# First batch of a spectral mixing layer: its transposes as whole 112 by 128 blocks and six steps ahead, the weights' sums on VectorE, half of y's writes on ScalarE's queue

## The chip, the core and the metric

The kernel runs on one core of one Trainium2 chip. The metric is device time in microseconds (us) for one execution. The engines named below are TensorE (PE, with PEld for its weight loads), VectorE (DVE), ScalarE (ACT), GpSimd (POOL) and SyncE (SP). SP, ACT and POOL also issue DMA transfers, each through a queue of its own.

## The reference

The reference filters a sequence in the frequency domain and passes the result through a two-layer network with an ELU between the layers. `x` (8 batches, 3008 steps, 256 channels) and the two filter parts (1505 frequencies, 256 channels) are float32. `w_in` (256 by 2048) and `w_out` (2048 by 256) are float64.

```python
X = np.fft.rfft(x, axis=1)
Y = X * (filt_r + 1j * filt_i)[None, :, :]
y = np.fft.irfft(Y, n=3008, axis=1).astype(np.float32)
h = y.reshape(8 * 3008, 256) @ w_in
g = np.where(h > 0.0, h, np.exp(np.minimum(h, 0.0)) - 1.0)
out = (g @ w_out).astype(np.float32)
```

## The kernel before

**The transform.** 3008 is 47 times 64, so each Fourier transform is done as matmuls in two steps with tables of cosines and sines. For a batch the stages are: first step (`a_*`), a change of layout, second step (`b_*`), the product with the filter, and the same two steps back (`bi_*`, `n_*`). Batches 1 to 7 change layout through a scratch tensor `z` in HBM. Batch 0 has functions of its own (`a_first`, `t_first`, `b_first`, `bi_first`) that change layout on chip by transposing with TensorE, so that the kernel can start without the round trip.

**The network.** The second layer's work is cut into 192 quads: for each of 8 batches, 6 blocks `m` of rows, and for each block 4 quarters `q` of the 2048 hidden channels. A quad does the "ups" (`w_in`, ELU) and, one quad later, the "downs" (`w_out`). All blocks but the first use seven products for a two by two block product, for which sums of weight blocks are needed (`w_sums`, L955: four dependent add or subtract operations of 128 by 256 each, for every second weight chunk; the last of the four overwrites the block `a21`). The first block of batch 0 (quads 0 to 3, `plain_ups` and `plain_downs`) does eight plain products and needs no sums; quad 4 is the first to read them, of `w_in[0]`, and quad 5's step reads those of `w_out[0]`.

**The weights.** They arrive as pairs of 32-bit words in 16 chunks (`w_fetch`), and are turned into float32 by DVE and ACT: `w_split` (L914, L915, two DVE operations), `w_float` (L925, three ACT operations), `w_join` (L929, L939, then L947 or L953, on DVE). The first chunks are converted during batch 0's transform, the rest during quads 0 to 3.

**The order.** The program is written out by hand (`manual_schedule`). Each engine works through its own list in order and waits on semaphores. What an engine does next is set by the order of the calls in the code. Batch 0's opening (from L977) is:

- loads of `x`, tables, the filter (`ff`, in two halves of eight rows: L1021 to L1024, on SP and POOL) and weights;
- `a_table` (DVE) and six `a_first`, with one warming matmul (`warm(1, 256)`, L1055, on data that nobody reads) after each of the first five;
- `t_first(0)`, `t_first(1)`, the first weight chunk (`step(0)`), `t_first(2)`, `t_first(3)`;
- a loop over g = 0 to 9 (L1065): `b_first(g)` for g below 8 with the four filter products on DVE (L407 to L410), `bi_first(g - 2)` in the middle of it from g = 2 on, `t_first(g + 4)` for g below 4, pieces of weight conversion at fixed g, and from g = 2 on `y_write_first(g - 2)`, two DMA transfers, one on SP's queue and one on POOL's (on ACT's for the last g);
- `y_read` (L1089, SP), the rest of the early weights, eight warming matmuls, and `n_unit(0, 0)`, with which the network begins.

`t_first(g)` (L332) writes four psum tiles in turn (`po0` to `po3`, two of them per g), each copied out by an ACT operation (L349). The destination `t` is one of `t2` (g 0 and 1), `t4p` (2 and 3) and `xp` (4 to 7); the last are the buffers in which `x` came. `b_first` takes two of the four banks `m0` to `m3` and gives them back after the products. `bi_first` uses `po0` to `po3` as well (L431).

Work at fixed points of the later quads is entered with `at(quad, place, function, ...)` (L1118). Within a quad the places come in the order 2, 3, 0, 4, 5, 1: 2 and 3 between its first seven steps, 0 in its middle, 4 and 5 between the last steps, 1 at its end. The weights' sums stand there (L1139), with POOL as engine, in quads 1 to 5. `x_unit` (L235) of batch 1, four DVE operations per pair of chunks, stands at place 0 of quads 3, 4 and 5; `a_unit` follows at place 1.

Of the kernel before, what the change touches and what calls it, by code (L numbers as in the profile page):

```python
# [11 lines left out]
FP32 = mybir.dt.float32  # L12
U32 = mybir.dt.uint32
AXT = mybir.ActivationFunctionType
# [12 lines left out]
P = 128  # L27
# [6 lines left out]
NXC = H // XC  # L34
NG = K2 // 4
# [3 lines left out]
HALVES = slice(0, 64), slice(64, 128)  # L39
# [103 lines left out]
def kernel(  # L143
# [9 lines left out]
    nc = tc.nc  # L153
# [6 lines left out]
    def pool(name, bufs, **kw):  # L160
        return ctx.enter_context(tc.tile_pool(name=name, bufs=bufs, **kw))
# [15 lines left out]
    psO = pool("psO", 1, space=PSUM)  # L177
# [105 lines left out]
    zt = [[], [w[3].rearrange("p a b c -> p (a b c)") for w in (w_in, w_out)]]  # L283
    ROWS = 112
# [32 lines left out]
    def a_first(c):  # L317
        xt, w = xs.pop((0, c)), tas.pop((0, c))
        for dh in range(2):
            k, ps = bank("psa", (P, 64, XC, 2))  # L320
            for u in range(XC):
                nc.tensor.matmul(ps[:, :, u, :], xt[:, u, ts(dh, P)], w[:, u, :].rearrange("p (k q) -> p k q", q=2),  # L322
                                 start=True, stop=True)
            for kh in range(2):
                z = zt[kh][dh]
                o = bass.AP(tensor=z.tensor, offset=z.offset + 2 * XC * c,
                            ap=[list(z.ap[0]), [ROWS, 16], [64, 2], [1, 2 * XC]])
                s = ps[:, 32 * kh:32 * kh + 32].rearrange("p (k a) u q -> p k a (u q)", a=2)
                nc.scalar.activation(out=o, in_=s, func=AXT.Copy)
            banks.append(k)  # L330

    def t_first(g):  # L332

        if g < 2:
            t = t2[:, g]
        elif g < 4:
            t = t4p.tile([P, 4, D], FP32, tag="t4", name="tf")
        else:
            t = xp.tile([P, 2, 2, D], FP32, tag="xc", name="tf").rearrange("p k u d -> p (k u) d")
        t2s[0, g] = t  # L340
        ps = [psO.tile([P, 4, 2, 64], FP32, tag="po%d" % i, name="po%d" % i) for i in range(2 * (g % 2), 2 * (g % 2) + 2)]
        for k in range(4):
            for dh in range(2):
                for o, n in ((0, 64), (64, ROWS - 64)):
                    for r, p in zip(HALVES, ps):
                        nc.tensor.matmul(p[o:o + n, k, dh, :], zt[k // 2][dh][r, (2 * g + k % 2) * ROWS + o:(2 * g + k % 2) * ROWS + o + n],  # L346
                                         eye[r, r], start=True, stop=True)
        for h, p in enumerate(ps):
            nc.scalar.activation(out=t[0:ROWS].rearrange("p k (e h f) -> p k e h f", e=2, h=2)[:, :, :, h], in_=p[0:ROWS], func=AXT.Copy)  # L349

# [59 lines left out]
    def b_first(g, f, pq, between):  # L412
        t = t2s.pop((0, g))
        (i0, re), (i1, im) = (bank(n) for n in ("psr", "psi"))
        for o, a in ((0, 0), (64, 2)):
            for ps, k in ((re, LO), (im, HI)):
                tile_mm(ps[o:o + 64], gf, k, [t[:, a:a + 2, :]], g == 0 and a == 0)
        if between:
            between()
        products(re, im, f, *pq)  # L420
        banks.extend((i0, i1))

        sr, si, p, q = pq
        ss[0, g] = [sr, p], [si, q]

    def bi_first(g):
        s = ss.pop((0, g))
        t = t3s[0, g] = (t2 if g % 4 > 1 else t3f)[:, g % 2]

        pa, pb = (psO.tile([P, 2, 256], FP32, tag="po%d" % i, name="po%d" % i)  # L430
                  for i in ((0, 1) if g > 2 and g % 2 else (2, 3)))  # L431
        for o, table, sv in ((0, gr, s[0]), (64, gi, s[1])):
            for ps, k in ((pa, LO), (pb, HI)):
                tile_mm(ps[o:o + 64], table, k, sv, g == 0 and k == LO)
        nc.scalar.activation(out=t[:, 0:2, :], in_=pa, func=AXT.Copy)
        nc.scalar.activation(out=t[:, 2:4, :], in_=pb, func=AXT.Copy)

    def y_write_first(g, queues=(nc.sync, nc.sync)):
        if g == 0:
            yds[0] = yd.tile([K2, 96, D], FP32, tag="yd", name="yd")  # L440
        t = t3s.pop((0, g))
        for a, r in enumerate((LO, HI)):
            queues[a].dma_start(yds[0][4 * g:4 * g + 4, 48 * a:48 * a + 48, :].rearrange("u r d -> r u d"), t[r])
# [467 lines left out]
    def w_split(k):  # L911
        m, e = wts[k] = wtmp[TEMPS[k]]
        hi = wds[k][:, :, 1]
        nc.vector.tensor_scalar(out=m, in0=hi, scalar1=0x000FFFFF, scalar2=None, op0=ALU.bitwise_and)  # L914
        nc.vector.tensor_scalar(out=e, in0=hi, scalar1=0x7FF00000, scalar2=None, op0=ALU.bitwise_and)  # L915

    def w_float(k, *parts):

        m, e = wts.get(k, (None, edges.bitcast(U32)))
        ef, l = e.bitcast(FP32), wds[k][:, :, 0]  # L920
        steps = [(l.bitcast(FP32), l, AXT.Identity, 2.0 ** -52, 1.0),
                 (ef, e, AXT.Relu, -8.0, edges[:, 0:1]), (e, ef, AXT.Relu, -1.0, edges[:, 1:2])]
        for i in parts or range(3):
            o, x, func, scale, bias = steps[i]
            nc.scalar.activation(out=o, in_=x, func=func, scale=scale, bias=bias)  # L925
# [51 lines left out]
    with tc.manual_schedule():  # L977


        with tc.tile_pool(name="boot", bufs=1) as bp:  # L980
            ff = bp.tile([P, 2, 2 * NG, D], FP32, name="ff")
            once = bp.tile([P, 2, P], FP32, name="once")
            eye, gf = once[:, 0], once[:, 1].rearrange("p (v q) -> p v q", v=2)
# [15 lines left out]
            def warm(n, w=512):  # L999
                ps = psO.tile([P, 512], FP32, tag="po3", name="warm")  # L1000
                for k in range(n):
                    nc.tensor.matmul(ps[:, 0:w], rq[:, 0, 0, 0:P], rq[:, 0].rearrange("p u d -> p (u d)")[:, 0:w], start=True, stop=True)
# [35 lines left out]
            k = kp.tile([P, 2, 2, 256], FP32, tag="k", name="wme").rearrange("p i u d -> p i (u d)")  # L1038
            places(k[:, 0], k[:, 1])
            c = kp.tile([P, 2, 512], FP32, tag="c", name="wme")  # L1040
# [3 lines left out]
            def step(k):  # L1044
                w_split(k)
                w_float(k)
                if k > 0 and k - 1 in wds:
                    w_join(k - 1)
# [2 lines left out]
                a_table(c)  # L1051
            for c in range(NXC):
                a_first(c)
                if c < NXC - 1:
                    warm(1, 256)  # L1055
            for g in range(2):
                t_first(g)
            step(0)
            for g in range(2, 4):
                t_first(g)  # L1060
            w_join(0)
            w_fetch(4, nc.gpsimd)
# [2 lines left out]
            for g in range(NG + 2):  # L1065
                back = (lambda g=g: bi_first(g - 2)) if g >= 2 else None
                if g < NG:
                    b_first(g, [ff[:, c, 2 * g:2 * g + 2] for c in range(2)], pqs[g % 2], back)
                else:
                    back()  # L1070
                if g < 4:
                    t_first(g + 4)
                if g == 1:
                    w_split(1)
                    w_float(1)
                if g == 2:
                    w_join(1)
                    w_fetch(5, nc.gpsimd)
                if g == 3:
                    w_split(2)  # L1080
                if 4 <= g < 7:
                    w_float(2, g - 4)
                if g == 6:
                    w_split(3)
                if g == 7:
                    w_float(3, 0)
                if g >= 2:
                    y_write_first(g - 2, (nc.sync, nc.scalar if g == NG + 1 else nc.gpsimd))
            y_read(0, 0, slice(0, K2 - 4), slice(K2 - 4, K2))  # L1089
            w_join(2)  # L1090
            w_fetch(6)
# [26 lines left out]
        def at(quad, place, fn, *a):  # L1118
            plan.setdefault((quad, place), []).append((fn, a))
# [16 lines left out]
        for quad, *counts in ((0, 1, 1, 1, 1, 1, 1, 1, 0), (1, 1, 1, 1, 1, 1, 1, 1, 1), (2, 1, 1, 1, 1, 1, 1, 1, 1), (3, 1, 1, 1, 0, 0, 0, 0, 0)):  # L1136
            for n, count in enumerate(counts):
                plan.setdefault((quad, 7 + n % 2, *BLOCKS[n // 2]), []).append((convert, (count,)))
        for quad, place, k in ((1, 2, 1), (2, 2, 3), (2, 0, 5), (3, 2, 7), (3, 0, 9), (4, 2, 11), (4, 0, 13), (5, 2, 15)):  # L1139
            at(quad, place, w_sums, k, nc.gpsimd)  # L1140
        for c, (quad, place) in enumerate(((2, 0), (2, 1), (2, 1), (2, 1))):
            at(quad, place, x_load, 1, c)
        at(0, 1, nc.sync.dma_start, pairs, pairs_d)
# [6 lines left out]
        for b in range(B):  # L1150
            t = (b - 1) * PER
# [109 lines left out]
```

## Time and profile before

| | us |
|---|---|
| median of 3 timed runs | 2559.62 |
| the three runs | 2555.52, 2559.62, 2561.19 |
| the profiled execution | 2552.35 |
| its span, from first to last instruction | 2550.5 |
| busy PE, PEld, DVE, ACT, POOL | 2520.4, 2167.4, 2105.0, 1509.4, 173.0 |

Busy times are shares of one execution; engines work side by side, so they do not add up. A gap of the engine that is on the path costs time, a gap of another engine does not. "Who waited for whom" names the engine and line that waited, what released it, the total in us, how often, and the longest wait. A table of windows gives for each stretch (us from the span's start) its length, then the busy time and the number of instructions of each engine, the granted TensorE clock (1.00 is full), the mean busy share of the DMA engines (about 1 is saturated) and GB/s. A timeline line gives start, duration, engine, line, operation, names, shape and count, and in brackets the idle time ahead of it and what ended it. L346 is line 346 of the kernel before.

### The profile page before, as it was taken

To read this page: it belongs to the slowest core of one execution; us is meant where nothing else is said; L and a number is where in the kernel's file an instruction comes from. 1 tells how busy PE (TensorE), PEld (TensorE's weight loads), DVE (VectorE), ACT (ScalarE), POOL (GpSimd) and SP (SyncE) were. 2 spreads that over 40 slices of the span, in tenths; PEclk is the share of its full clock that TensorE was granted. 3 is DMA by queue.
4 is the path that set the end of the run, shared out by engine and by line. 5 is a ranking of instruction groups with operands and counts; after the bars stand their busy time and mean duration, and the time that the engine had idled before them with its cause. 6 is when DMAs were issued, how large, how long until landed. Compare 5 with 4: busy or idle time off the path is not lost.

```text
span 2550.5 us, 46325 instructions
## 1 busy us (share of the span) xinstructions
PE 2520.4 (99%) x17766; PEld 2167.4 (85%) x17766; DVE 2105.0 (83%) x3607; ACT 1509.4 (59%) x2652; POOL 173.0 (7%) x325
## 2 busy tenths in 40 slices
PE   7899999999999999999999999999999999999999
PEld 5788889888898888988889888888889888898887
DVE  4968897888888888888888898788897888876766
ACT  4755565656556565565555656556655665555554
POOL 3310000000000000000000000000010001000000
PEclk9999999999999999999999999999999999999999
DMA  8653213512234232342224321343223322111010
GB/s 205 198 158 83 57 42 88 135 47 72 47 86 120 58 73 54 91 101 66 59 51 124 86 71 36 77 116 82 57 48 91 83 53 69 38 45 29 9 28 17
DMA packets 226671, 194.43 MB, mean 76 GB/s; under 512 B 127914, under 2 KB 199306, under 8 KB 226258
## 3 DMA queue, kind: packets, MB, share of 16 engines
q1 hardware_dynamic: 212722, 161.39, 25.8%
q0 software_dynamic: 13232, 29.62, 4.2%
q8 instruction: 140, 2.29, 0.4%
q14 instruction: 81, 0.66, 0.1%
q10 hardware_dynamic: 496, 0.46, 0.1%
HBM read 119.51 MB, written 74.97 MB: 76 GB/s over the span
## 4 chain that ended last, share of the span: by engine, by line
PE 95%; DVE 2%; DMA 1%; issue 1%; ACT 1%; SPq 1%; POOL 0%; ACTq 0%; DVEq 0%; POOLq 0%
PE po L816 44%; PE phs L730 25%; PE phd L730 12%; PE pha L730 6%; PE psn L608 2%; PE pf L458 1%; PE pv L525 1%; PE psa L254 1%; PE po L402 1%; PE po L690 0%; SPq L866 0%; PE po L346 0%; PE psa L322 0%; DMA t<-tf_t 0%; PE psr L402 0%
## 5 line engine op out<-in xcount | busy, mean ns | idle before, releaser
L816 PE MATMUL po<-g,wo 128*128 128x256 f32 (+1 forms) x5264 | 1293.8, 377 | 0.0
L816 PEld LDWEIGHTS po<-g,wo 128*128 128x128 f32 x5264 | 990.8, 190 | 165.3 <-issue 51.7
L741 ACT ACTIVATE g<-phs 128x512 f32<-128x512 f32 (+1 forms) x564 | 332.2, 589 | 743.4 <-PE phs L730 743.3
L748 ACT ACTIVATE e<-e 128x512 f32<-128x512 f32 (+1 forms) x752 | 468.1, 623 | 23.9
L738 DVE TENSOR_TENSOR g<-phd,g 128x512 f32<-128x512 f32 (+1 forms) x376 | 254.4, 677 | 198.7 <-ACT e L748 120.0
L752 DVE SCALAR_TENSOR_TENSOR g<-e,g 128x512 f32<-128x512 f32 (+1 forms) x564 | 380.2, 674 | 14.2 <-ACT e L748 14.1
L730 PE MATMUL phs<-y,wi 128*128 128x256 f32 (+1 forms) x1504 | 380.0, 375 | 0.0
L730 PE MATMUL phd<-y,wi 128*128 128x256 f32 (+1 forms) x1488 | 376.0, 375 | 0.4 <-DVE g L738 0.4
L747 ACT ACTIVATE e<-g 128x512 f32<-128x512 f32 (+1 forms) x564 | 347.1, 615 | 36.0 <-DVE g L738 29.2
L730 PEld LDWEIGHTS phs<-y,wi 128*128 128x128 f32 x1504 | 285.6, 190 | 33.0
L730 PEld LDWEIGHTS phd<-y,wi 128*128 128x128 f32 x1488 | 282.2, 190 | 33.7 <-DVE g L738 0.8
L752 DVE SCALAR_TENSOR_TENSOR g<-e,phs 128x512 f32<-128x512 f32 (+1 forms) x188 | 127.2, 677 | 87.2 <-ACT e L748 87.2
L730 PE MATMUL phs<-yb,wi 128*128 128x256 f32 (+1 forms) x752 | 190.2, 375 | 0.3 <-ACT g L741 0.3
L730 PE MATMUL phs<-yt,wi 128*128 128x256 f32 (+1 forms) x752 | 190.0, 375 | 0.0
L730 PE MATMUL pha<-yb,wi 128*128 128x256 f32 (+1 forms) x736 | 185.9, 375 | 0.0
L747 ACT ACTIVATE e<-phs 128x512 f32<-128x512 f32 (+1 forms) x188 | 110.1, 585 | 114.5 <-PE phs L730 114.5
L396 POOL DMA_DIRECT2D fall<-fp x224 | 110.1, 499 | 805.5 <-DVE r L502 797.8
L730 PEld LDWEIGHTS phs<-yb,wi 128*128 128x128 f32 x752 | 140.4, 190 | 19.6 <-ACT g L741 0.7
L738 DVE TENSOR_TENSOR g<-pha,g 128x512 f32<-128x512 f32 (+1 forms) x188 | 126.9, 675 | 36.4 <-PE pha L730 36.4
L730 PEld LDWEIGHTS phs<-yt,wi 128*128 128x128 f32 x752 | 142.8, 190 | 16.5
L730 PEld LDWEIGHTS pha<-yb,wi 128*128 128x128 f32 x736 | 139.8, 190 | 16.1
L791 DVE TENSOR_TENSOR g<-g,g 128x512 f32<-128x512 f32 (+1 forms) x188 | 128.2, 682 | 6.5
(170 smaller groups left out, 2217.6 us busy)
## 6 DMA issues: line engine op xcount, KB each, us to landing
yd<-t SPq DMA_DIRECT2D x120, 192.0 KB
fall<-fp POOLq DMA_DIRECT2D x224, 96.0 KB, 2.9
t<-z SPq DMA_DIRECT2D x224, 96.0 KB
t<-yd SPq DMA_DIRECT2D x84, 256.0 KB
out_dram<-o SPq DMA_DIRECT2D x624, 32.0 KB
z<-t SPq DMA_DIRECT2D x144, 128.0 KB
xc<-in_x_dram SPq DMA_DIRECT2D x84, 128.0 KB
xc<-in_x_dram SPq DMA_DIRECT2D x161, 64.0 KB
```

The lines of the kernel that those rows point to most:

```text
L254: nc.tensor.matmul(ps[k][1][a:a + 32, u, :], w[r, u, 32 * o:32 * o + 32], parts[o][r, u, :], start=True, stop=True, tile_position=(32 * k, a))
L396: nc.gpsimd.dma_start(t[32 * a:32 * a + 24].rearrange("p c u d -> p (c u d)"), fp[g, a].rearrange("q c u d -> q (c u d)"))
L402: nc.tensor.matmul(ps[:, u:u + w, :], table[k, v, :], r[k, u:u + w, :], start=n == 0, stop=n == len(rhs) - 1)
L608: nc.tensor.matmul(o, t[r, i - 4 * m, ds(dh * P + 64 * c, 64)], w[r, i - 4 * m, :], start=True, stop=True)
L730: nc.tensor.matmul(ps[:, a, 0:h], w_in[q][:, COMBO[n], a, :], y[n], start=start and a == 0, stop=True, skip_group_check=True)
L738: nc.vector.tensor_tensor(out=g[o], in0=i0, in1=i1, op=ALU.add)
L741: nc.scalar.activation(out=g[o], in_=i0, func=AXT.Copy)
L747: nc.scalar.activation(out=e, in_=src, func=AXT.Relu, scale=-1.0)
L748: nc.scalar.activation(out=e, in_=e, func=AXT.Exp, scale=-1.0)
L752: nc.vector.scalar_tensor_tensor(out=g[n], in0=es[n], scalar=1.0, in1=src, op0=ALU.subtract, op1=ALU.max)
L791: nc.vector.tensor_tensor(out=b12, in0=b22, in1=b12, op=ALU.subtract)
L816: nc.tensor.matmul(po[i][:, u, 0:h], w_out[q][:, COMBO[n], a, :], g[n][:, a, :], start=q == 0 and a == 0 and n in (1, 3, 6, 4), stop=True, ...
```

## The change

`t_first` transposes a whole block of 112 columns by 128 partitions with one instruction, against the full identity, where it multiplied eight pieces of at most 64 by 64 with a corner of the identity each. For every g that is 8 calls in place of 32. Each psum tile now holds one of the two halves `j`, and ACT copies it out as it stands.

`t_first(0)` to `t_first(5)` are called ahead of the loop (`t_first(0)` to `t_first(3)` before), so the loop's calls are `t_first(6)` and `t_first(7)`. The five warming matmuls between the `a_first` are left out. The second DMA of `y_write_first` goes to ACT's queue for every g. The weights' sums are done by DVE, at other places: quads 3, 4 and 5 only.

```diff
-        ps = [psO.tile([P, 4, 2, 64], FP32, tag="po%d" % i, name="po%d" % i) for i in range(2 * (g % 2), 2 * (g % 2) + 2)]
-        for k in range(4):
-            for dh in range(2):
-                for o, n in ((0, 64), (64, ROWS - 64)):
-                    for r, p in zip(HALVES, ps):
-                        nc.tensor.matmul(p[o:o + n, k, dh, :], zt[k // 2][dh][r, (2 * g + k % 2) * ROWS + o:(2 * g + k % 2) * ROWS + o + n],
-                                         eye[r, r], start=True, stop=True)
-        for h, p in enumerate(ps):
-            nc.scalar.activation(out=t[0:ROWS].rearrange("p k (e h f) -> p k e h f", e=2, h=2)[:, :, :, h], in_=p[0:ROWS], func=AXT.Copy)
+        for j in range(2):
+            i = j + 2 * (g % 2)
+            ps = psO.tile([P, 2, 256], FP32, tag="po%d" % i, name="po%d" % i)
+            for u in range(2):
+                for dh in range(2):
+                    nc.tensor.transpose(ps[0:ROWS, u, ts(dh, P)], zt[j][dh][:, ts(2 * g + u, ROWS)], eye)
+            nc.scalar.activation(out=t[0:ROWS, 2 * j:2 * j + 2, :], in_=ps[0:ROWS], func=AXT.Copy)
...
                 a_first(c)
-                if c < NXC - 1:
-                    warm(1, 256)
             for g in range(2):
                 t_first(g)
             step(0)
-            for g in range(2, 4):
+            for g in range(2, 6):
                 t_first(g)
...
-                if g < 4:
-                    t_first(g + 4)
+                if g < 2:
+                    t_first(g + 6)
...
-                    y_write_first(g - 2, (nc.sync, nc.scalar if g == NG + 1 else nc.gpsimd))
+                    y_write_first(g - 2, (nc.sync, nc.scalar))
...
-        for quad, place, k in ((1, 2, 1), (2, 2, 3), (2, 0, 5), (3, 2, 7), (3, 0, 9), (4, 2, 11), (4, 0, 13), (5, 2, 15)):
-            at(quad, place, w_sums, k, nc.gpsimd)
+        for quad, place, k in ((3, 4, 1), (3, 1, 3), (3, 0, 5), (4, 2, 7), (4, 0, 9), (4, 1, 11), (5, 2, 13), (5, 0, 15)):
+            at(quad, place, w_sums, k)
```

## The prediction

> **What bounds the kernel now.** Read first the page (PE is busy 2520.4 of 2550.5 us), then a table of windows by stage:
>
> ```profile
> 0.00:24.20 24.20, 19.22 (x123) 15.00 (x123) 9.24 (x29) 12.59 (x26) 10.32 (x21) 1.00 0.95 239
> 24.20:35.40 11.20, 4.64 (x248) 4.23 (x249) 2.75 (x5) 5.26 (x10) 5.35 (x10) 0.89 1.03 214
> 35.40:71.30 35.90, 32.37 (x473) 19.05 (x465) 25.83 (x44) 17.85 (x32) 6.97 (x12) 0.89 0.62 172
> ...
> 81.30:133.20 51.90, 45.97 (x242) 43.76 (x243) 46.34 (x77) 35.40 (x62) 23.56 (x26) 1.00 0.57 186
> 133.20:190.00 56.80, 54.49 (x410) 44.78 (x410) 36.20 (x59) 35.25 (x63) 7.40 (x13) 1.00 0.62 165
> 190.00:2550.00 2360.00, 2354.61 (x16257) 2035.75 (x16255) 1974.88 (x3378) 1394.54 (x2449) 117.75 (x242) 1.00 0.28 67
> ```
>
> From 190 us on PE has 5 us free in 2360 and the change leaves that work alone, so the answer lies in the first 190 us. What PE waits for there (PE alone, 0 to 200):
>
> ```profile
> PE po L346 <- issue: 9.1, 3, 5.8
> PE php L663 <- DVE g L672: 4.9, 4, 1.9
> ...
> PE phd L730 <- DVE g L738: 2.0, 1, 2.0
> ...
> PE php L663 <- DVE wi L947: 1.0, 1, 1.0
> ```
>
> The largest has no semaphore behind it: PE stands inside `t_first` with nothing to wait for. Windows cut at these stalls:
>
> ```profile
> 26.30:28.95 2.65, 2.40 (x128) 2.13 (x128) 0.00 (x0) 2.02 (x5) 2.44 (x5) 1.00 0.88 224
> 28.95:34.70 5.75, 0.00 (x0) 0.00 (x0) 1.99 (x3) 2.01 (x4) 1.77 (x4) 0.85 1.07 219
> 34.70:40.75 6.05, 5.96 (x128) 4.47 (x128) 2.80 (x5) 2.17 (x4) 1.73 (x4) 0.58 1.05 208
> 40.75:43.40 2.65, 0.00 (x0) 0.00 (x0) 2.65 (x6) 0.00 (x0) 0.00 (x0) 0.96 0.97 365
> ```
>
> Exactly 128 matmuls and 128 weight loads run between one stall and the next, with the DMA engines full. The DMA view counts one "q8 instruction" packet in 23.4 to 25, one in 29 to 34 and one in 40.7 to 43.4, and the page's queue part gives 2.29 MB over 140 packets, 16 KB each. I read this as PE running out of instructions, whose next block queues behind data. The stalls also cost clock: 0.58 in the third row. [...]
>
> **The change part by part: the opening.** Before, each g has 32 calls of four records (two passes, load and multiply): 512 of each over eight g. The last lines of the kernel (L877) have 8 transposes of 128x128 as 8 matmuls and 8 loads, so one pass. After: 64 of each, 896 instructions fewer, 3.5 blocks. Time: four of L877 take 0.79 us with a 0.29 us tail, 0.15 us apart; a g costs 8 x 0.15 = 1.2 us against 1.7 for its 64 records in 23.65 to 25.3. ACT's copies stay at two of 0.59, 1.1 us a g.
>
> Counting PE and PEld records from the start (246 by 24.2 us), the first stall comes after 449. After, the six `a_first` end at 221, six t_first add 96, and 449 comes in `bi_first(0)`, about 37 us, with its block asked for some 16 us earlier. The next is 256 later, five steps of the loop (48 records each), about 13 us. A block took at most 8 us (from 26.4, when the previous one began, to 34.8). So I expect no stall: 9.1 us go, and the half clock.
>
> What is late next is the filter. Its transfers are on POOL's queue, which the change does not touch until the loop:
>
> ```profile
> 23.97 0.59 POOL L389 DMA_DIRECT2D ff<-in_filt_i_dram  x1 [1.17 <-DMA ff<-in_filt_i_dram]
> ...
> 32.46 0.57 POOL L389 DMA_DIRECT2D ff<-in_filt_i_dram  x1 [1.41 <-DMA ff<-in_filt_i_dram]
> ```
>
> The first half's last transfer goes out at 23.97, and the issue at 32.46 is released by it: 32.5 is the earliest for the first L408. PE is there sooner. x's chunks arrive every 1.8 us (POOL's issues at 13.02 to 19.88 wait for them). `a_first` takes 1.78 us without the 0.43 us of warming and ends near 22; ACT then has 12 copies and 2 us of `w_float`, so t_first(5) and `b_first(0)` are through near 31. Whatever `a_first` and the transposes win is hidden behind the filter.
>
> ```profile
> 37.49 0.69 DVE L407 TENSOR_TENSOR rq<-psr,ff 128x512 f32<-128x512 f32 x1 [5.42 <-PE psi L402]
> ...
> 68.67 0.68 DVE L410 TENSOR_TENSOR zq<-psi,ff 128x512 f32<-128x512 f32 x1
> ```
>
> Products run from 37.49 to 69.27. After: first products to 34.3 (three more at 0.6 after 32.5); then DVE has 7 x 2.4 us, two splits and one more at 0.67 each, one join at 1.9: 34.3 + 16.8 + 2.0 + 1.9 = 55.0. PE's step is 2.57 (58.65, 61.20, 63.80 for L407) and keeps ahead, since the t_first are nearly gone from the loop. Later steps follow as before: last products to `psn` 9.6 us (69.27 to 78.87), then `php` at 81.32. That is 14.2 us; I take **13.5**, 0.1 us a step for semaphores. Unseen is when weights and the second half of the filter land. Floor: the DMA engines are empty from 48 to 50 (0 GB/s), so by 47.5 all has landed; chunk 2 is needed at 44, which costs up to 3.5. Ends: 10 and 14.5.
>
> ACT's queue: each y transfer costs ACT 0.37 us (72.00, L443), 7 new ones 2.6 us, on an engine busy 17.85 of 35.9. Queued behind are the next copies and `w_float`; PE has two psum pairs to wait on, from g = 3 on, so nothing on the path. If they were, 2.6. POOL loses its seven issues, on nobody's path. The warming: row 9.04:12.45 has PE busy 1.48 of 3.41 and the clock held; row 39.77:43.18 has 0.96 and the next slice shows 0.50.
>
> ```profile
> 9.04:12.45 3.41, 1.48 (x12) 1.07 (x10) 2.19 (x11) 1.32 (x4) 0.73 (x1) 1.00 1.05 290
> 39.77:43.18 3.41, 0.96 (x28) 0.55 (x20) 2.96 (x7) 0.51 (x2) 0.00 (x0) 1.00 0.97 333
> 44.00:46.00 2.00, 2.00 (x42) 1.15 (x35) 0.00 (x0) 1.02 (x3) 0.00 (x0) 0.50 0.80 312
> ```
>
> Without the warming of 9.92 the first has about 0.9, so the clock may halve for the 3.4 us after it: 1.5 us, which fits in the 1.4 to 1.5 us ahead of the filter. [...]
>
> **The sums off POOL.** No engine waits for L962; POOL's memset L230 and its transfers L396 stood behind the sums and can only come earlier. But in quads 0 to 3 DVE's operations beside it are longer:
>
> ```profile
> 95.85 0.94 DVE L914 TENSOR_SCALAR wme<-wd 128x512 uint32<-128x512 uint32 x1
> ...
> 101.38 0.42 DVE L914 TENSOR_SCALAR wm<-wd 128x512 uint32<-128x512 uint32 x1
> ```
>
> Some 17 such operations between 87 and 133, 0.5 us each: 8 to 9 us of DVE. PE's stalls there are 4.9 + 1.0 = 5.9, five of them. Two (0.54, 1.21) and the one behind L947 (0.97) end with inflated operations and go; 1.87 loses 0.5; 1.32 follows a `psn` that holds two banks and stays. **3.0**, between 0 and 5.9.
>
> **The sums on DVE.** 32 operations of 128x256; L620 does the like in 0.42, four in 1.7 us: 13.4 us in all. DVE's idle times there are 4.12 ahead of 138.46, 2.27 ahead of 144.08 and 5.78 ahead of 159.22. Quad 3's three groups (k = 5, 1, 3; 5.1 us) fill the first, and the x_unit there runs 1.35 us shorter without POOL. k = 7 and 9 and the x_unit queue ahead of L738 on `phd`: 139.1 + 3.4 + 2.7 = 145.2 against 144.08, done at 145.8, and PE wants the bank at 145.43: 0.4 us and a semaphore. k = 11, 13, 15 (5.1) fit into 5.78. **0.5 lost**, between 0 and 13.4 (all of it on the path).
>
> Sum: 13.5 + 3.0 - 0.5 = **16.0 less**. The profiled execution goes from 2552.35 to 2536.3. That execution lies 7.3 us under the median of the timed runs; against the median, 2559.62 - 16.0 = **2543.6**.
>
> **The rivals.** Time against the median.
> (a) DVE becomes the bound in quads 3 to 5: all 13.4 us on the path, 13.5 + 3.0 - 13.4 = 3.1 less, 2556.5. For it: 46.34 of 51.9 busy up to 133; against: 36.20 of 56.8 after.
> (b) The loop stays tied to loads: only its start moves: 5 + 3.0 - 0.5 = 7.5 less, 2552.1. For it: DMA near 1.05 until 40; against: 0 GB/s at 48.
> (c) The stall isn't what I think and stays: 9.1 less won, 2552.7. Against: 128 and 128.
> (d) The other side: without the warming PE falls to half clock at 12.8 and stays there. Full-rate PE work from there to `bi_first(7)` is about 8.9 + 9.6 + 20 = 38.5; at half rate the opening ends at 89.8 in place of 71.3, 18.5 later, less 2.5: 2575.6. Slower from about 45 us of half rate on; the trace has 10 in all.
>
> **How the numbers follow.** Forecast 0.68, (a) 0.10, (b) 0.08, (c) 0.06, (d) with whatever else costs more than it brings 0.08. 0.2% is 5.1 us, about what the three runs can tell from no change. Faster: 0.68 + 0.08 + 0.06 and a little of (a), 0.84; same: most of (a), 0.08; slower: 0.08. The bounds give 14.5 + 5.9 = 20.4 less (2539) and 10 + 0 - 13.4 = 3.4 more (2563); runs lie up to 4 us off their median. I leave (d) and the far end out: 2536 to 2557. The forecast's own range is 2538 to 2550.
>
> **What would show it.** Right: no "issue" stall at L346; first L407 at 31 to 33, last L410 near 55; `php` near 68; L914 at 0.42 throughout; a stall of under 1 us before L730 `phd` in quad 4. Wrong: a long wait of the products for `ff` or of L914 for a chunk; PE stalls at L730 of several us in quads 3 to 5; the clock at 0.5 past 20 us.

## The result, and the profile after

The changed kernel takes 2537.85 us (median of four runs, 2535.93 to 2538.45) against 2558.74 us for the kernel before, measured beside it (2555.52 to 2561.19): a ratio of 0.9918, with a 95% interval of 0.9901 to 0.9935. Its profiled execution takes 2535.93 us, with a span of 2533.8; before's were 2552.35 and 2550.5. The sum of the prediction was made on the profiled execution: 16.0 less, against 16.4 measured. Between the medians the change is 20.9 us.

Line numbers of shared code are two lower than before (L407 to L410 became L405 to L408, L663 became L661). First the windows of the kernel after, by stage, with the columns of the prediction's first table:

```profile
0.00:24.20 24.20, 20.41 (x133) 16.32 (x134) 9.09 (x29) 14.86 (x30) 11.13 (x22) 1.00 0.96 241
24.20:35.40 11.20, 7.86 (x68) 4.86 (x67) 6.81 (x12) 8.57 (x16) 4.55 (x8) 1.00 1.00 201
35.40:71.30 35.90, 34.86 (x228) 18.98 (x227) 33.04 (x64) 22.91 (x40) 2.22 (x4) 1.00 0.91 276
```

In 24.2 to 35.4 PE now has 68 matmuls in place of 248, and the clock is at 1.00 where it was 0.89. In the third row VectorE is busy 33.0 of 35.9 us (25.8 before). In the loop, from the first product to the last, it now stands idle for 0.75 us of 24.27 (waits of 0.26 and 0.28 for PE, 0.21 for DMA), so it sets the pace there, though PE shows no wait either. What PE waits for up to 200 us, in the kernel after:

```profile
PE po L346 <- ACT tf L347: 3.3, 1, 3.3
PE php L661 <- DVE g L670: 2.3, 2, 1.3
PE phd L728 <- DVE g L736: 2.0, 1, 2.0
...
PE psa L273 <- DVE g L670: 0.5, 1, 0.5
```

The 9.1 us with no releaser are gone from the first place. There is a new wait of 3.3 us in `t_first` (whose transposes stand on L346 too), with a cause: ScalarE has not copied an earlier psum tile out. The five stalls at `php`, 5.9 us, have become two of 2.3. One of 0.5 us is new, and the 2.0 us at `phd` are as before. The products, in the timeline of VectorE of the kernel after (start, duration):

```profile
31.33 0.69 DVE L405 TENSOR_TENSOR rq<-psr,ff 128x512 f32<-128x512 f32 x1 [1.69 <-PE psi L400]
...
54.92 0.68 DVE L408 TENSOR_TENSOR zq<-psi,ff 128x512 f32<-128x512 f32 x1
```

They run from 31.33 to 55.60; before, from 37.49 to 69.35. Laying marks on both traces divides the whole difference:

| stretch | before | after | difference |
|---|---|---|---|
| start to first product | 37.49 | 31.33 | -6.16 |
| first product to end of the last | 31.86 | 24.27 | -7.59 |
| to the first `php` (network begins) | 11.97 | 11.93 | -0.04 |
| to the first `psa` L273 (`a_unit`, quad 3) | 51.87 | 47.60 | -4.27 |
| to the first `phd` (quad 4) | 9.75 | 10.59 | +0.84 |
| to the end | 2407.61 | 2408.11 | +0.50 |

So 13.8 us come from the opening, and 2.9 from what the sums' move gave (4.27) and took (1.34).

### The profile page after: what moved, and what is told of

Same layout as the page of the kernel before. It is cut to its first block, busy times and chain, and to the rows that moved or that the text cites. A ratio compares the mean times of both kernels' runs of the same rounds, so it can differ in the third digit from the quotient of the medians.

```text
span 2533.8 us, 45395 instructions
## 1 busy us (share of the span) xinstructions
PE 2514.7 (99%) x17308; PEld 2160.6 (85%) x17308; DVE 2104.8 (83%) x3639; ACT 1509.0 (60%) x2652; POOL 140.7 (6%) x286
## 4 chain that ended last, share of the span: by engine, by line
PE 93%; DMA 2%; DVE 2%; SPq 1%; ACT 1%; issue 0%; ACTq 0%; DVEq 0%
PE po L814 44%; PE phs L728 25%; PE phd L728 12%; PE pha L728 6%; PE psn L606 2%; PE pf L456 1%; PE pv L523 1%; PE psa L254 1%; DMA fall<-in_moe_w_in_dram 1%; SPq L864 0%; PE po L400 0%; DMA t<-yd 0%; DMA fall<-in_moe_w_out_dram 0%; ACT wme L923 0%; DMA wd<-in_moe_w_in_dram 0%
## 5 line engine op out<-in xcount | busy, mean ns | idle before, releaser
L814 PEld LDWEIGHTS po<-g,wo 128*128 128x128 f32 x5264 | 990.8, 190 | 165.3 <-issue 51.7
L736 DVE TENSOR_TENSOR g<-phd,g 128x512 f32<-128x512 f32 (+1 forms) x376 | 254.1, 676 | 197.0 <-ACT e L746 120.3
L750 DVE SCALAR_TENSOR_TENSOR g<-e,g 128x512 f32<-128x512 f32 (+1 forms) x564 | 379.5, 673 | 14.5 <-ACT e L746 14.3
L736 DVE TENSOR_TENSOR g<-pha,g 128x512 f32<-128x512 f32 (+1 forms) x188 | 126.7, 674 | 33.6 <-PE pha L728 33.6
```

What stands on the lines that cost most here:

```text
L736: nc.vector.tensor_tensor(out=g[o], in0=i0, in1=i1, op=ALU.add)
L750: nc.vector.scalar_tensor_tensor(out=g[n], in0=es[n], scalar=1.0, in1=src, op0=ALU.subtract, op1=ALU.max)
L814: nc.tensor.matmul(po[i][:, u, 0:h], w_out[q][:, COMBO[n], a, :], g[n][:, a, :], start=q == 0 and a == 0 and n in (1, 3, 6, 4), stop=True, ...
```

## Experiments

### Whole transposes alone

The run `whole_only`: the kernel before with only `t_first` changed; order, warming, sums and queues of before.

```diff
...
-                        nc.tensor.matmul(p[o:o + n, k, dh, :], zt[k // 2][dh][r, (2 * g + k % 2) * ROWS + o:(2 * g + k % 2) * ROWS + o + n],
-                                         eye[r, r], start=True, stop=True)
...
+                    nc.tensor.transpose(ps[0:ROWS, u, ts(dh, P)], zt[j][dh][:, ts(2 * g + u, ROWS)], eye)
...
```

> The kernel before with one edit: the first batch's transposes whole; their order in the loop, the warming, the sums on POOL and y's queues stay. Theory (PE stood still because its instruction blocks of 256 came late, and 896 fewer instructions mean that no block is needed before about 37 us): the wait 'po L346 <- issue' of 9.1 us is gone, the first product is bound by the filter's last first-half transfer and starts at 31.5 to 33 us (37.49 before), the opening gains 12 to 13.5 us, and the clock shows no 0.5; 2539 to 2543 profiled (before 2552.35). Rival (the gain of the opening comes from transposing six steps ahead, so that the loop has less to do for each step): less than half, 5 us or less, 2547 or more, with the loop's step still set by the transposes in it.

Measured: 2541.97 us (2541.05 to 2543.47), ratio 0.9951 [0.9931, 0.9970] to before's 2553.36 beside it. In the profile (2541.82) no wait at `po` is without a releaser (PE, 20 to 60 us):

```profile
PE psr L400 <- DVE rq L406: 0.9, 1, 0.9
PE po L346 <- ACT t L433: 0.7, 1, 0.7
PE po L346 <- ACT tf L347: 0.5, 1, 0.5
```

The last product ends at 57.47, 11.9 us earlier than in before (12 to 13.5 expected). That is nearly all of the opening's 13.8, so the rival (the order of the calls wins) falls. The clock is at full in the opening; one halved stretch of 3.4 us comes later, at 152.4. What now holds the first products is seen on VectorE of the same kernel:

```profile
30.55 0.68 DVE L405 TENSOR_TENSOR rq<-psr,ff 128x512 f32<-128x512 f32 x1
32.38 0.69 DVE L406 TENSOR_TENSOR rq<-psr,ff 128x512 f32<-128x512 f32 x1 [1.16 <-DMA ff<-in_filt_i_dram]
```

The first product, at 30.55, is earlier than expected. The second waits for the filter and starts at 32.38, the 32.5 that the prediction read from POOL's queue.

### The 64x64 tiles in the new order

The run `tiles_kept`: the kernel after, with before's body of `t_first`, so everything else of the change and the old tiles.

```diff
...
-                    nc.tensor.transpose(ps[0:ROWS, u, ts(dh, P)], zt[j][dh][:, ts(2 * g + u, ROWS)], eye)
...
+                        nc.tensor.matmul(p[o:o + n, k, dh, :], zt[k // 2][dh][r, (2 * g + k % 2) * ROWS + o:(2 * g + k % 2) * ROWS + o + n],
+                                         eye[r, r], start=True, stop=True)
...
```

> The kernel after, but with the 64x64 tiles of before in the transposes, six steps ahead of the loop. Theory (blocks of instructions): the six transposes ahead make about 900 records before the first b_first instead of about 610, so three stalls of the sizes before (0.6, 5.8, 2.7) fall ahead of the first product, which starts at 40 to 45 us, later than before's 37.5; the opening gains nothing or loses up to 5 us, and with the 2 to 2.5 us of the sums on VectorE the time is 2547 to 2555 (after 2535.9 profiled). Rival (order is what wins): the first product at 33 to 36 us and at least half of the 13.8 us stay, 2543 or less.

Measured: 2553.27 us, ratio 0.9998 [0.9981, 1.0015]. All of the gain is gone. PE, 20 to 60 us:

```profile
PE po L346 <- issue: 14.3, 3, 6.0
```

The first product starts only at 49.64, later than the 40 to 45 expected, because the stalls came to 14.3 us and the clock stood at 0.5 from 31.2 to 51.7. The loop after it is then as short as the changed kernel's (24.58 us), since six transposes are out of it.

### As many instructions with whole transposes

The run `padded`: `whole_only` with 28 more 64x64 multiplications for each g ahead of the transposes, whose results are overwritten; a g issues 64 matmuls and 64 weight loads, as before.

```diff
...
+        for n in range(14):
+            for r, p in zip(HALVES, both):
+                nc.tensor.matmul(p[0:64, 0, 0:64], zt[0][0][r, 2 * g * ROWS:2 * g * ROWS + 64], eye[r, r], start=True, stop=True)
...
```

> Whole transposes in the order of before, with 28 further 64x64 multiplications for each g ahead of them that nobody reads, so that a g has as many instructions for TensorE as before (64 and 64) though the transposes are whole. Theory (the number of instructions decides): the stalls with no releaser are back, 5 to 14 us of them, 256 records apart, first product at 36 us or later, 2548 to 2558. Rival (the 64x64 tiles or their copies were slow by themselves, the number is beside the point): only the 0.7 us or so of PE time for each g, no stall over 1 us, first product by 33.5, 2543 to 2546.

Measured: 2559.06 us (2553.89 to 2560.58), 1 us above the expected range, ratio 1.0013 [0.9994, 1.0032]; first product at 39.82. The stall is back, but only one, of 2.2 us where 5 to 14 were expected. PE, 20 to 60 us:

```profile
PE po L344 <- issue: 2.2, 1, 2.2
```

A padded g takes PE 2.79 us (t_first(0) at 23.47, the next at 26.26). That is 1.1 more than before's 1.7, and 1.9 more than the 0.87 of a g in `whole_only`, not the 0.7 I had allowed for. So PE reaches the end of a block later and the block has more time to come. Eight padded g come to some 15 us (an estimate, 8 times 1.9) of the 17.4 by which this profile's span is longer than that of `whole_only`. Most of the loss is thus the padding's own work, and the total settles nothing; the padding is itself of 64x64 tiles, too. What speaks for the number of instructions is the place: the stall stands behind 40 of 56 like multiplications. Here is where PE stood still in `t_first` without a releaser, in every kernel profiled with the small tiles, padded or not. All records of PE's queue are counted from the start: matmuls, weight loads and the 13 to 17 of its semaphores and drains. (Waits without a releaser of up to 0.8 us at `psn`, in some profiles, are left out: other profiles name a DMA load there.)

| kernel | after record 449 | after 705 | after 961 | first product | last product ends |
|---|---|---|---|---|---|
| before | 0.56 | 5.84 | 2.71 | 37.49 | 69.35 |
| before, second profile | 1.73 | 6.65 | 2.70 | 38.46 | 70.74 |
| before, third | 0.36 | 6.38 | 3.37 | 36.92 | 71.85 |
| before, fourth | 1.07 | 6.65 | 2.18 | 40.56 | 74.24 |
| sums on VectorE alone (below) | 1.18 | 6.38 | 3.78 | 37.72 | 72.64 |
| small tiles, new order | 4.07 | 6.02 | 4.16 | 49.64 | 74.22 |
| padded | none | 2.24 | none | 39.82 | 73.08 |
| small tiles, less data (below) | 1.29 | 4.74 | none | 35.41 | 63.07 |
| whole transposes alone | none | none | none | 30.55 | 57.47 |
| after | none | none | none | 31.33 | 55.60 |

Three records, 256 apart, whatever stands there: record 961 comes behind two `b_first` in before and ahead of the first one with small tiles in the new order. By matmuls and weight loads alone the places would differ (436 in before, 432 with small tiles in the new order, which has four more semaphore records by then); with all records they are the same.

The DMA records tie the stalls to the instruction packets of queue q8. In each of the 21 stalls of this table PE goes on 1.3 to 1.8 us after such a packet has landed. For the largest of before, the packet starts at 32.03 and lands at 33.36; PE:

```profile
34.77 0.48 PE L346 MATMUL po<-once,wo 64*64 64x64 f32 x8 [5.84 <-issue]
```

With whole transposes the packet that starts ahead of record 449 has landed at 25.6 in the kernel after and at 25.5 in `whole_only`, and PE passes that record at 37.0 and 38.5, some 11 and 13 us later. There are as many packets as blocks of 256 records (140 in before, 136 in the kernel after), and in these two kernels each starts between 4.4 us before and 6.2 us after PE enters the block ahead of it.

### Less data moving

The run `light`: the kernel before, with the filter's second half left out (the products of g = 4 to 7 multiply by zeros) and five weight chunks and the twiddles fetched later.

```diff
-            for k in range(0, 16, 8):
+            for k in range(0, 8, 8):
...
-            w_fetch(2)
-            w_fetch(3)
-            tn_read(0, 0)
...
-            w_fetch(4, nc.gpsimd)
-            for k in (7, 8):
-                w_fetch(k, nc.gpsimd)
...
+                if g == 2:
+                    w_fetch(2)
+                    w_fetch(3)
+                    tn_read(0, 0)
+                    w_fetch(4, nc.gpsimd)
+                    for k in (7, 8):
+                        w_fetch(k, nc.gpsimd)
```

> The kernel before with its 64x64 tiles and as many instructions, but with less data moving while it transposes: the second half of the filter is not loaded (the products of g = 4 to 7 use zeros), and two weight chunks of SyncE's queue, three of POOL's and the twiddles are asked for only when the first y has been written, at about 50 us. Only the stretch up to the first product is read. Theory (the blocks of instructions queue behind data): the blocks come within 1.5 to 4 us of being asked for and the stalls come to less than 3.5 us together. Rival (a block takes its 6 to 8 us whatever else moves): stalls of 8 us or more.

Measured: stalls of 6.0 us, between the two expectations; the four profiles of before have 9.1 to 11.1. The data had not stopped by then. Windows of this kernel, the last but one column being the DMA engines' busy share:

```profile
25.40:27.95 2.55, 2.39 (x128) 2.12 (x128) 0.00 (x0) 1.92 (x4) 0.00 (x0) 1.00 0.90 163
27.95:32.69 4.74, 0.01 (x1) 0.00 (x0) 1.99 (x3) 2.02 (x4) 0.00 (x0) 0.85 0.32 97
33.00:40.00 7.00, 7.00 (x180) 5.03 (x172) 3.95 (x7) 2.70 (x6) 0.00 (x0) 0.64 0.02 5
```

The first two stalls lie where transfers still run or have just ended; the third stall, 2.2 to 4.2 us in before and in small tiles with the new order, is not there, in a stretch with a share of 0.02. The starts of the instruction packets say the same: 22.38, 30.27, 33.78, 37.78 here, so 7.9 us apart across the busy stretch and then 3.5 and 4.0; before has 23.55, 32.03, 40.99, 44.54, so 8.5 and 9.0 apart while the share is about 1, and 3.6 when it falls. From one packet to the next it thus took 3.5 to 4.0 us in these two kernels while the share fell and after it, and 7.9 to 9.0 us behind data. "6 to 8 us whatever else moves" is out; "gone with less data" is too much. The share alone does not tell the length, though. In before the packets at 32.03 and 40.99 start 5.7 and 6.2 us after PE has entered the block ahead (shares 1.02 and 1.04), the one at 44.54 only 1.1 us after (0.77), but in this kernel the one at 30.27 starts 4.9 us after at 0.78. Which transfers hold a packet was not separated.

### The sums, both ways

`sums_kept` is the kernel after with the weights' sums on POOL in their old places, `sums_only` the kernel before with the sums on VectorE in the new ones.

```diff
-        for quad, place, k in ((3, 4, 1), (3, 1, 3), (3, 0, 5), (4, 2, 7), (4, 0, 9), (4, 1, 11), (5, 2, 13), (5, 0, 15)):
-            at(quad, place, w_sums, k)
+        for quad, place, k in ((1, 2, 1), (2, 2, 3), (2, 0, 5), (3, 2, 7), (3, 0, 9), (4, 2, 11), (4, 0, 13), (5, 2, 15)):
+            at(quad, place, w_sums, k, nc.gpsimd)
```

> The kernel after, but with the weights' sums on POOL in the places of before. Theory (two separate gains): the opening is that of after, psn at 65 us and the first php near 67.5; the plain stage to quad 3 is that of before, with stalls of about 5.4 us instead of 3.2, VectorE's op L912 at 0.9 instead of 0.42, so 2 to 2.5 us more than after: 2538 to 2538.5 profiled. Rival (the later gain comes with the earlier opening, not with the sums): the same time as after within 0.7.

> The kernel before, with the weights' sums alone moved to VectorE, to the places of after. Theory: 'po L346 <- issue' stays at about 9 us, psn stays at 78 to 79 us, the first psa L273 comes 2 to 2.5 us earlier than before's 133.2: 2549.8 to 2550.5 profiled (before 2552.35). Rival (the sums' move is worth nothing alone, or costs a wait of the kind of after's 0.54 us psa L273 <- DVE g L670): 2552 or more.

`sums_kept`: 2541.85 us (2539.03 to 2543.04), ratio 0.9961 [0.9939, 0.9982]; profiled 2539.03, 3.1 above after's. Its products end at 55.90, as in after. From the first `php` to the first `psa` L273 it takes 51.87 us, as in before, against after's 47.60. PE, 60 to 130 us:

```profile
PE php L661 <- DVE g L670: 4.9, 4, 1.9
...
PE php L661 <- DVE wi L945: 1.0, 1, 1.0
```

These are before's stalls again. The sums are worth 3.1 us here (3.4 by the spans) and not 2 to 2.5, so the two gains are separate.

`sums_only`: 2553.28 us against 2553.36, ratio 1.0000 [0.9986, 1.0014]: the total shows nothing. Its profile has 47.62 us between the same two marks, so the 4.3 us are won here too, but its stalls at `po` came to 11.3 us instead of 9.1, its first `php` stood 3.3 us later than in before's first profile, and a halved clock of 3.4 us fell on quad 5. One profile and ten times can't show 3 us on a kernel whose own times spread by 19. The rival's number came true, and for a reason that it did not give.

### Why the times of before spread

On one chip the kernel before took 2543 to 2562 us. These are three more profiles of it.

> The kernel before once more, for a second profile of it. Its times on one chip spread over 2543 to 2562 us, where kernels with whole transposes spread over 2 to 4 us. Theory (the spread is in the opening: the blocks of instructions come late by a different time in each execution, and each stall halves the clock for a while): the waits 'po L346 <- issue' differ from the 9.1 us of the first profile in the same direction as the span does, and from the first php to the end the two profiles agree within 2 us. Rival (the spread comes from later work): equal stalls in the opening, and the difference after it.

> A third profile of the kernel before, for the same question, with the same expectations.

> A fourth profile of the kernel before. In its timed runs the time goes with the granted clock: 2543 to 2544 at 0.999 to 1.0, 2551 to 2554 at 0.997, 2559 to 2562 at 0.993 to 0.995, which is about what the lost clock comes to by itself (0.001 of 2550 is 2.5 us). Theory (stalls for instruction blocks in the opening, and the halved clock that follows them, make the spread): whatever the time of this execution, stalls end at records 449, 705 and 961, and a fast execution near 2544 shows stalls of less than 5 us together and at most one halved window. Rival: a fast execution with stalls of 9 us or more and a full clock.

The four spans are 2550.5, 2552.4, 2555.9 and 2558.5 us. The stalls at `po` do not follow them (9.1, 11.1, 10.1 and 9.9 us), against the expectation. Up to the first `php` the four take 81.3, 82.7, 83.8 and 86.2 us, and from there to the end 2469.2, 2469.7, 2472.1 and 2472.3: of the 8 us, 5 lie in the opening and 3 behind it, where agreement within 2 us was expected. The granted clock does follow the spans: its mean is 0.998, 0.997, 0.995 and 0.994. Windows of the fourth profile (the column behind POOL is the clock):

```profile
33.70:43.90 10.20, 6.05 (x117) 4.40 (x121) 3.12 (x5) 2.17 (x4) 2.66 (x5) 0.50 1.02 214
47.30:54.20 6.90, 6.90 (x49) 3.69 (x41) 0.69 (x1) 3.00 (x6) 0.00 (x0) 0.51 0.21 80
115.60:119.00 3.40, 3.40 (x11) 3.04 (x10) 3.26 (x9) 2.26 (x4) 0.00 (x0) 0.50 0.86 214
170.20:173.60 3.40, 3.40 (x12) 2.17 (x14) 2.74 (x6) 2.52 (x4) 0.00 (x0) 0.50 0.10 24
```

Each begins during or just after a PE stall: the two blocks, the 1.9 us at `php`, the 2.4 us at `phd`; so does a fifth, from 13.2 us, behind a wait of 2.4 us at `psa`. Between 5 and 180 us the four profiles have 10.2, 13.7, 23.9 and 27.3 us at half clock. Half of that taken off leaves 2545.4, 2545.6, 2543.9 and 2544.9, so 8 us of spread become 1.6. This is an estimate: it takes PE as busy at half clock throughout, and in the first row it was for 6.05 of 10.2 us. The halved stretches came in lengths of 3.4, 6.8 and 10.2 us, and the stall of 1.9 us at `php` was followed by one in two of these four executions and not in the others; why was not shown. No profile fell on an execution near 2543, whose mean clock was 0.999 to 1.0: that it has shorter block stalls is likely from its clock and was not seen.

This is also the likely reason why the timed medians differ by 20.9 us and the profiled executions by 16.4: before's first profile has the least half clock of the four (5.1 us by the same reckoning, none after), and its other executions have more.

### The parts that were given no price

The run `rest_back`: the kernel after with the warming put back and y's second half on POOL again, beside the kernel after on the same chip.

```diff
                 a_first(c)
+                if c < NXC - 1:
+                    warm(1, 256)
...
-                    y_write_first(g - 2, (nc.sync, nc.scalar))
+                    y_write_first(g - 2, (nc.sync, nc.scalar if g == NG + 1 else nc.gpsimd))
```

> The changed kernel with the two parts that were given no price taken back: the five warming multiplications stand between the a_first again, and y's second half goes out on POOL's queue again. Theory (both are worth nothing): the first product within 0.5 us of after's 31.3, the time within 0.7 us of after. Rival (the warming, 5 times 0.43 us, is on the path of the opening): first product 1 to 2 us later and the time 1 to 2 us longer.

> The changed kernel once more, on the same chip as the next two, to compare them by. Its time is 2536 to 2541: 2536 to 2538 where the stall of 1.98 us at phd in quad 5 leaves the clock alone, 1.7 more where a halved window of 3.4 us falls on it.

Measured: 2538.32 us (ratio 0.9938 [0.9918, 0.9959]) for `rest_back` and 2538.72 us (ratio 0.9940 [0.9919, 0.9962]) for the kernel after beside it. First products at 32.65 and 32.25, last ones end at 56.62 and 56.22. The first product is thus later than the expected 31.3 in both, and 0.4 us later with the two parts taken back. Both together are worth less than the spread. The six transposes ahead have a price only in the profile: `sums_kept`, which has them, ends its products at 55.90, `whole_only` at 57.47, though the two differ in the warming and in y's queue as well; their median times are 2541.85 and 2541.97.

### A version that takes two waits away

After's 2.0 us at `phd` in quad 5 were in before too. VectorE in the kernel after, there:

```profile
138.04 1.67 DVE L960 TENSOR_TENSOR wo<-wo 128x256 f32<-128x256 f32 x4
142.31 0.69 DVE L634 SCALAR_TENSOR_TENSOR yb<-y,y 128x512 f32<-128x512 f32 x1 [2.61 <-ACT y L611]
...
143.38 0.68 DVE L238 TENSOR_TENSOR sd<-xc 128x512 f32<-128x512 f32 x1
...
146.03 0.68 DVE L736 TENSOR_TENSOR g<-phd,g 128x512 f32<-128x512 f32 x1
```

VectorE idles 2.61 us because `n_sums` (L634) needs ScalarE, then does 2.7 us of `x_unit` (L238, L239), and PE waits for L736 behind it. The run `better` turns them round, so that `x_unit` fills the idle time. The new 0.5 us at `psa` came from the sums of k = 1 ahead of the last `elu` of quad 3; they go to its end.

```diff
-        for quad, place, k in ((3, 4, 1), (3, 1, 3), (3, 0, 5), (4, 2, 7), (4, 0, 9), (4, 1, 11), (5, 2, 13), (5, 0, 15)):
+        for quad, place, k in ((3, 1, 1), (3, 1, 3), (3, 0, 5), (4, 2, 7), (4, 0, 9), (4, 1, 11), (5, 2, 13), (5, 0, 15)):
...
+        plan[5, 0].sort(key=lambda e: e[0] is n_sums)
```

> The changed kernel with two waits taken on: the four x_unit operations of quad 5 stand ahead of n_sums instead of behind it (VectorE stands idle there for 2.6 us, waiting for ScalarE), and the sums of k = 1 stand at the end of quad 3 instead of ahead of the last elu of the quad. Theory: the 1.98 us at phd go, and with them the halved clock windows there, and the 0.54 us at psa of quad 3 go with the 0.85 us that quad 3 to 4 takes more than before: 2 to 3 us below after, 2533 to 2535.5, and a spread of under 2 us. Rival (x has not landed by then, or the sums are then late for the next quad): the wait stays as one for DMA or for wi, within 0.7 us of after.

Measured: 2533.85 us (2533.38 to 2536.48), ratio 0.9922 [0.9898, 0.9945] to before, where the kernel after has 2538.72 and 0.9940 beside it: 4.9 us less, and the best of all here. VectorE of this version in the same stretch:

```profile
139.08 0.68 DVE L238 TENSOR_TENSOR sd<-xc 128x512 f32<-128x512 f32 x1
...
141.77 0.69 DVE L634 SCALAR_TENSOR_TENSOR yb<-y,y 128x512 f32<-128x512 f32 x1
...
142.84 0.68 DVE L736 TENSOR_TENSOR g<-phd,g 128x512 f32<-128x512 f32 x1
```

L736 starts at 142.84 instead of 146.03, and no wait at `phd` or at `psa` L273 is left in the first 200 us. From the first `psa` L273 to the first `phd` it takes 9.75 us, as before the change (after 10.59), and from there to the end 2406.60 (after 2408.11). These two are 2.35 us. The medians differ by more; the likely reason, not shown by a profile of these two kernels, is that the halved stretch behind the wait went with it. In the profiles of `whole_only` and `sums_only` one of 3.4 us began right behind it, at 152.4 and 165.2. The spread came to 3.1 us, not under 2.

## Why the prediction was right, point by point

**The opening, 13.5: measured 13.8.** The reading held: PE stood waiting for a block of 256 instructions. The stalls lie behind records 449, 705 and 961, the same in five kernels, and each ends 1.3 to 1.8 us behind a landed packet. Whole transposes issue so few instructions that PE passes record 449 without a stall, 11 us behind its packet in the kernel after; small tiles bring the stalls back in the new order (14.3 us). In each kernel profiled with small tiles, padded or not, the costliest crossing took between 2.24 us (`padded`, in a stretch with a DMA share of 1.09) and 6.65 us (before, second and fourth profiles).

Some readings of the prediction were loose, without effect on the sum. Its 449 counts all records of PE's queue, while the 246 beside it are matmuls and loads alone. A block took 8.4 us by its own marks, not 8, and packets start up to 9.5 us apart in other profiles. A whole-transposed g takes PE 0.87 us, not 1.2. Record 449 came at 37.0 us, as forecast.

Inside the term two sizes were off and cancelled, which is luck. PE's part was to be through near 31 and the filter to hold the products until 32.5. In `whole_only` the filter does (32.38). In the kernel after PE's part came at 31.33, as forecast, and the filter was there by then. POOL's issue that its last first-half transfer releases stood at 32.46 in before; here it is

```profile
31.45 0.56 POOL L387 DMA_DIRECT2D ff<-in_filt_i_dram  x1 [1.94 <-DMA ff<-in_filt_i_dram]
```

and the second product, to which the 32.5 belongs, starts at 31.94 without a wait for it. PE's own path has a step that was priced by its work alone: the weight chunk's `w_float` stands between the copies of `t_first(1)` and `t_first(2)` on ScalarE and waits for its data.

```profile
25.32 0.68 ACT L923 ACTIVATE fall<-fall 128x512 f32<-128x512 uint32 x1 [1.49 <-DMA fall<-in_moe_w_in_dram]
26.12 1.48 ACT L923 ACTIVATE wme<-wme,edges 128x512 f32<-128x512 uint32 x2
27.50 3.98 ACT L347 ACTIVATE tf<-po 112x512 f32<-112x512 f32 x8
```

This is the timeline of ScalarE in the kernel after: eight copies of `t_first` queue behind a wait for DMA, and PE, whose next psum tiles are not free, stands for 3.3 us. That the last `a_first` ended at 20.7 and not near 22 made up for it. The loop then took 24.27 us where the sum has 22.5 (32.5 to 55.0): the fourth product of the first g (0.6; the sum starts at the second product), splits of 0.76 in place of 0.67 (0.3), and three small waits (0.26, 0.28 and, at chunk 2, 0.21 for DMA). Of the 3.5 us set aside for loads, 0.21 came.

**Sums off POOL, 3.0: measured 4.27.** Three stalls went as expected, and 1.87 became 1.34, as expected too. The step that failed is "1.32 stays": it became 0.92. So 3.65 of the 5.9 went; 0.6 more lies between the marks outside PE's waits, and where was not traced. L912 is at 0.42 us throughout, as expected (0.94 beside POOL's sums before).

**Sums on VectorE, 0.5 lost: measured 1.34.** The place was wrong. I expected the wait at `phd` in quad 4 behind k = 7 and 9; that came to 0.3 us without a wait to be seen. Larger was quad 3: I had put all three groups of it into the idle 4.1 us ahead of `pha`, but place 4 comes ahead of the quad's last `elu`, and so k = 1 kept PE's bank for 0.54 us. The two errors of the sums, 1.27 and 0.84 us, cancel to 0.4 by luck: 2.9 net against 2.5.

**ACT's queue and warming, nothing:** `rest_back` shows both at nothing. The halving of 3.4 us that the prediction allowed for without the warming (in before one lasts 3.41 us, from 43.18) did not occur in the kernel after's first profile and did, between 12.8 and 17.5 us, in the four others without the warming (and once in nine with it). With whole transposes the first product then lies at 31.54 to 32.25 against 31.33. I had it hidden; whether the up to 0.9 us are its cost was not separated, as `rest_back`, with the warming and a full clock there, has 32.65.

**The rivals.** (a), VectorE as the bound in quads 3 to 5, is refuted by the 1.34 us, though VectorE is now the bound in the opening's loop. (b), the loop tied to loads, is refuted: 0.21 us. (c), a stall of another kind, is refuted by `whole_only`. (d), half clock through the opening: not after; but the kernel with small tiles in the new order shows that such a state exists, 20 us of it, and there it can cost up to 10 us (an estimate, half of it).

**Against the median.** 16.0 was subtracted from 2559.62, as if the 7.3 us between the profile and the median stayed. By the four profiles they belong to the clock of the kernel before, and mostly went with its stalls, so the median came 5.8 us lower than forecast. It lies just below the forecast's own range, 2538 to 2550, and the 20.9 us between the medians are more than the 20.4 that the bounds allow. The time lost to the clock is a term that the sum did not have.

## What to carry to other kernels

A PE stall that no semaphore explains, at equal distances in PE's records and with full DMA engines, was here a matter of how many instructions are issued; fewer and larger ones helped more than their own time says (11.9 us in `whole_only`, where eight g at 0.87 us of PE in place of 1.7 make 6.6, an estimate). The packets of the instruction queue show it directly. Before a median is compared with a sum made on one profile, see how much half clock that profile has: stalls of 1.9 to 2.9 us were followed here, in some executions, by 3.4 us at half clock. And when work moves to another engine's queue, look for that engine's idle time ahead of a wait, and put independent work before the instruction that waits, not behind it.

## What was not expected of the hardware

In five kernels the stalls fell behind records 449, 705 and 961 and nowhere else, whatever the instructions. Around these stalls packets of instructions started 8.2 to 9.5 us apart with the DMA engines full (8.5 and 9.0 in before's first profile, at shares of 1.04 and 1.03), and 3.5 to 3.6 us apart both at a share of 0.08 (`light`) and at 0.89 (before). A PE stall of 1.9 to 2.9 us was followed by 3.4 us at half clock in some executions (at 113.5 and 168.1 us in one profile of before, at neither place in another), while the 3.3 us of the kernel after at 24.8 left the clock at 1.00.
